# A fused spectral-mixing and GeGLU kernel: loads of x shared between two issuing engines, new instruction orders, and a separate key for the last half tile

## The chip, the cores and the metric

The kernel runs on one core of a Trainium2 chip. The metric is the time of one execution on the device, in microseconds (us). Three runs of the kernel before took 491.49, 491.52 and 491.66 us (median 491.52). A profile of one execution gives the start and length of the instructions on each engine: TensorE (PE, with its weight loads as PEld), VectorE (DVE), ScalarE (ACT), GpSimd (POOL) and SyncE (SP, which here only starts transfers).

## What is computed

```python
h  = x + irfft2(rfft2(layernorm(x)) * (w_r + 1j * w_i))        # over tokens and channels
h2 = h + (gelu(layernorm(h) @ w_gate) * (layernorm(h) @ w_up)) @ w_down
```

x has 2048 tokens of 576 channels in bf16; w_gate and w_up are 576 x 4608, w_down is 4608 x 576. The layer norms have no weights. The Fourier transforms are done as matrix products with cos/sin tables that are constants of the program.

## The kernel before

The 2048 tokens lie in 16 tiles of 128 rows (c = 0 to 15; token 16p + c is row p of tile c). The work goes through these stages, and TensorE goes from one to the next.

**Stage A** (tokens to frequencies, first factor). Tile by tile, x is loaded (`x_load`), its mean and variance are taken, and the transform's table is multiplied by 1/std, so that the matmuls need no normalized x. The tiles are handled in six groups, `GROUPS` (line 23): tiles 0-1, 2-3, 4-6, 7-9, 10-12, 13-15. For a group the chain is:

- statistics of each tile: on DVE two half-tile `bn_stats` (tokens `B` and `b` in the order list, line 480) and then `bn_aggr` (`v`, line 489); for tiles 3, 4 and 13 on ACT instead, a sum (`S`, line 472) and a sum of squares (`Q`, line 476), with the mean squared by a small instruction `m` (line 483) on POOL or DVE;
- the square root on ACT (`q`, line 496) and the reciprocal on DVE (`c`, line 501);
- the scaled table ATS = ATB * 1/std (`x`, line 506 on POOL or 511 on DVE);
- a negated copy of the upper half of x (`n`, line 553) and a copy of its middle (`t`, line 558), both on POOL;
- the matmuls (`M`, line 537; 9 for each tile) and their evictions from PSUM to U (`E`, and `F` for the second half of a split one, line 548).

The order of all these instructions is written by hand in one list, `SEQ1` (line 24). Each token emits its instructions on one engine (the ending A, D or P names ACT, DVE or POOL), and each engine runs its own in the order in which they stand in the list and waits in place for what an instruction needs. `k` tokens are idle matmuls on zeros.

**The loads** come ahead of it, in the order of `LORD` (line 25): `x0-2` loads tiles 0 and 1 of x, `a0-4` tiles 0 to 3 of the table ATB. All are issued by SP. A trailing `@` would have ACT issue one (line 434); no entry has it. After them SP issues FT and BT, the spectral weights WS (22 transfers), VT and the tables of later stages, and then feed-forward weights. ACT's first instruction is a small square root (line 431, key `("SA0", 0)`), for which it loads its table.

**Stages D, B, T, Z, V, R** (the channel transform, the spectral product and the way back) go over 16 groups of frequencies in the order `SEQF` (line 28): D and B are matmuls with an eviction on ACT, `w` and T and Z the products on DVE, V and R matmuls with evictions on ACT and DVE. **Stages I and N** bring six token tiles back and add them to x; squares, reciprocals, the normalized HN (`n`, `e`), the transposes by PE (`A` evicted by ACT, `D` by DVE, `z` by both) and the first pieces of the gate and up products (`g`, `h`) are ordered by `SEQ` (line 31). `I` has its eviction on ACT, and `J` is an `I` with its eviction on DVE; `S` is the square on DVE and `s` the same on ACT.

**The feed-forward** goes over four blocks of 512 tokens: `gu_part` (line 877, gate and up) and then `down` (line 978) for the block's four tiles. `down` does a tile in two pieces of columns, 0-288 and 288-576, for the last tile 0-448 and 448-576. Each piece is 36 matmuls, one addition on DVE into OS (line 981) and one store by SP (line 983). OS has two buffers, used in turn.

Dependencies are found by keys: an instruction names the keys that it reads and writes, and `emit` (line 226) makes a wait for each earlier instruction on another engine, or on its own (except PE), that it has to follow. An instruction with two waits has one of them as a separate instruction in its queue (line 288). In the last tile the first addition writes the keys `("OS", 1, 0)` and `("OS", 1, 1)`, since 448 columns reach over the usual border of 288; the second writes `("OS", 1, 1)`.

Of the kernel before, what the change touches and what calls it, by code (L numbers as in the profile page):

```python
# [9 lines left out]
S, D, K2 = 2048, 576, 289  # L10
# [5 lines left out]
NT = 16  # L16
# [296 lines left out]
def _build(nc, A_x, A_w_r, A_w_i, B_w_gate, B_w_up, B_w_down, out):  # L313
    P = Prog(nc)
    T = build_tables()
    dram = {n: nc.inline_tensor(_np_bf16(T[n]), name="c_" + n.lower()) for n in T}
    PE, DVE, ACT, SP, POOL = "pe", "dve", "act", "sp", "pool"
# [4 lines left out]
    XO = sb.alloc("XO", [128, NT, D], BF16)  # L322
# [645 lines left out]
    def down(tb, p):  # L968
        c = 4 * tb + p

        cut = 448 if c == NT - 1 else 288
        for h, (d0, d1) in enumerate(((0, cut), (cut, D))):
            b = 2 * (tb > 0 and p % 2 == 0) + h
            for k, f in enumerate([*range(36)] if tb == 0 else [*range(9, 36), *range(9)]):
                if tb == 0:
                    for fn in DEF.get(72 * p + 36 * h + k, ()):
                        fn()
                P.op(PE, lambda t, b=b, d0=d0, d1=d1, f=f, p=p: t.matmul(bank(b, 0, 128, 0, d1 - d0), AT[:, f, 128 * p:128 * p + 128],  # L978
                                                                        WD[:, f, d0:d1], start=(f == 9 * (tb > 0)), stop=(f == (8 if tb else 35))),
                     r=[("AT", f), ("WD", f // 4)], w=[("PS", b)])  # L980
            P.op(DVE, lambda v, b=b, d0=d0, d1=d1, p=p, c=c: v.tensor_tensor(OS[:, p % 2, d0:d1], bank(b, 0, 128, 0, d1 - d0), XO[:, c, d0:d1], op=ALU.add),  # L981
                 r=[("PS", b), ("X", c)], w=[("OS", p % 2, k) for k in (range(2) if d1 == cut and cut > 288 else (h,))])
            P.dma(SP, ov[:, c, d0:d1], OS[:, p % 2, d0:d1], f"so{p % 2}{h}", r=[("OS", p % 2, h)], w=[("OUT", p % 2, h)])
# [65 lines left out]
```

## Time and profile before

| what | value |
|---|---|
| median of three runs | 491.52 us |
| the profiled execution | 491.4 us, its span in the profile 489.6 us |
| PE busy | 482.3 us (99% of the span) |
| ACT, DVE, POOL busy | 151.4, 192.8, 32.9 us |
| granted TensorE clock | 1.00 throughout |
| stage A's last run of matmuls | 15.00 to 19.84 us |
| D, B, V, R matmuls | 19.84 to about 48 us |
| I, N and the transposes | 48.04 to 58.95 us |
| feed-forward | 58.95 to 486.64 us |
| end of the last addition | 487.38 us |

Landing of the first loads, each from its issue and the time from issue to landing that the transfer view gives:

| load | issued | lands after | landed |
|---|---|---|---|
| x0-2 (288 KB) | 0.73 | 2.9 | 3.63 |
| x2-4 (288 KB) | 1.18 | 3.2 | 4.38 |
| a0-4 (128 KB) | 1.64 | 3.0 | 4.6 |
| x4-8 (576 KB) | 2.11 | 5.4 | 7.52 |
| a4-8 (128 KB) | 2.58 | 6.0 | 8.6 |
| x8-12 (576 KB) | 3.06 | 7.1 | 10.2 |
| x12-16 (576 KB) | about 3.5 | 8.1 | 11.6 |
| a8-16 (256 KB) | 4.01 | 8.3 | 12.3 |
| FT (432 KB) | 4.70 | 9.2 | 13.9 |

Times in the profile are counted from the start of the span. In a row of the timeline the first number is the start, the second the length; the bracket at the end tells how long the engine was idle before it and what ended that. The chain of waits follows the work that ended last back to its start.

### The profile page before, as it was taken

What the parts mean: (1) busy time and instruction counts of PE and PEld (TensorE: products, weight loads), DVE (VectorE), ACT (ScalarE), POOL (GpSimd) and SP (SyncE); (2) the same over time, 40 slices, a digit from 0 to 9 for tenths busy, and PEclk for the clock granted to TensorE, in tenths of its full rate; (3) what the DMA queues carried; (4) which work ended last, traced back from release to release, by engine and by line L of the source; (5) the groups of instructions that cost most, each with busy time, mean ns of one, the idle gap of its engine ahead of it and who ended that gap; (6) DMA issues with size and microseconds to landing.
All of it is one profiled execution on the core that took longest, in us unless ns stands there. A gap on an engine that the chain in (4) does not pass through costs nothing.

```text
span 489.6 us, 9943 instructions
## 1 busy us (share of the span) xinstructions
PE 482.3 (99%) x4376; PEld 286.2 (58%) x4376; DVE 192.8 (39%) x392; ACT 151.4 (31%) x297; POOL 32.9 (7%) x67
## 2 busy tenths in 40 slices
PE   7999999999999999999999999999999999999997
PEld 3887754444688744444577644444677444444774
DVE  6799733433576534433311144333211233333101
ACT  6999742332322223233200022332100123223000
POOL 6411431000000020000000000000000000000000
PEclk9999999999999999999999999999999999999999
DMA  8991999000001071100000001000000000000000
GB/s 289 224 328 20 365 362 345 19 15 2 1 19 40 14 233 26 23 2 1 2 18 19 13 20 23 15 1 0 7 19 19 7 1 0 1 2 1 13 19 19
DMA packets 25148, 31.20 MB, mean 64 GB/s; under 512 B 11440, under 2 KB 17840, under 8 KB 25104
## 3 DMA queue, kind: packets, MB, share of 16 engines
q1 hardware_dynamic: 22208, 18.62, 13.4%
q0 software_dynamic: 2896, 11.95, 7.0%
q8 instruction: 34, 0.56, 0.5%
q14 instruction: 10, 0.08, 0.1%
HBM read 26.22 MB, written 2.36 MB: 58 GB/s over the span
## 4 chain that ended last, share of the span: by engine, by line
PE 96%; DVE 1%; DMA 1%; ACT 0%; SPq 0%; issue 0%; POOL 0%; DVEq 0%
PE PS L877 57%; PE PS L978 29%; PE PS L611 2%; PE PS L621 2%; PE PS L651 1%; DMA XO<-in_A_x_dram 1%; PE PS L895 1%; PE PS L537 1%; PE PS L736 1%; DVE ST L480 1%; PE PS L779 1%; PE PS L913 1%; PE PS L841 0%; SPq L223 0%; PE PS L663 0%
## 5 line engine op out<-in xcount | busy, mean ns | idle before, releaser
L877 PE MATMUL PS<-HT,WG 64*128 64x512 bf16 (+1 forms) x2160 | 228.7, 371 | 0.0
L877 PEld LDWEIGHTS PS<-HT,WG 64*128 64x128 bf16 x2160 | 104.7, 94 | 122.2 <-issue 0.7
L886 DVE TENSOR_TENSOR AT<-GL,PS 128x512 bf16<-128x512 bf16 (+1 forms) x147 | 99.4, 677 | 177.9 <-ACT GL L885 177.9
L885 ACT ACTIVATE GL<-PS 128x512 bf16<-128x512 f32 (+1 forms) x147 | 86.5, 589 | 262.6 <-PE PS L877 251.3
L978 PE MATMUL PS<-WD,AT 128*128 128x288 bf16 (+2 forms) x1152 | 144.9, 286 | 0.0
L978 PEld LDWEIGHTS PS<-WD,AT 128*128 128x128 bf16 x1152 | 110.7, 98 | 30.6 <-ACT GL L885 1.3
L877 PE MATMUL PS<-HT,WGX 64*128 64x512 bf16 x486 | 53.4, 376 | 0.0
L981 DVE TENSOR_TENSOR OS<-PS,XO 128x288 bf16<-128x288 f32 (+2 forms) x32 | 14.6, 457 | 94.8 <-PE PS L978 94.7
L877 PEld LDWEIGHTS PS<-HT,WGX 64*128 64x128 bf16 x486 | 23.7, 94 | 28.8
L611 PE MATMUL PS<-FT,U 128*128 128x288 bf16 x96 | 13.9, 286 | 0.0
L630 DVE TENSOR_TENSOR TP<-YS,WS 128x1152 bf16<-128x1152 bf16 (+2 forms) x17 | 12.0, 718 | 2.8 <-ACT YS L603 2.6
L900 ACT ACTIVATE EB<-PS 128x288 f32<-128x288 f32 x10 | 4.1, 411 | 27.7 <-PE PS L895 27.7
L480 DVE BATCH_NORM_STATS2 ST<-XO 128x6 f32<-128x288 bf16 x26 | 10.0, 440 | 3.6 <-DMA XO<-in_A_x_dram 3.6
L918 DVE TENSOR_TENSOR XO<-PS,XO 128x576 bf16<-128x576 f32 x10 | 7.6, 756 | 8.0 <-PE PS L913 8.0
L537 PE MATMUL PS<-ATS,XO 128*128 128x128 bf16 x96 | 8.5, 219 | 2.3 <-POOL ATS L506 2.3
L611 PEld LDWEIGHTS PS<-FT,U 128*128 128x128 bf16 x96 | 9.3, 98 | 2.4
L603 ACT ACTIVATE CUS<-PS 128x576 bf16<-128x576 f32 x16 | 10.5, 654 | 0.5
L603 ACT ACTIVATE YS<-PS 128x576 bf16<-128x576 f32 x16 | 10.4, 654 | 0.1
L621 PE MATMUL PS<-CUS,BT 128*128 128x288 bf16 x64 | 10.3, 286 | 0.0
L548 ACT ACTIVATE U<-PS 128x384 bf16<-128x384 f32 (+2 forms) x29 | 9.5, 429 | 0.2
L906 DVE TENSOR_TENSOR QB<-PS,EB 128x288 f32<-128x288 f32 x20 | 8.2, 452 | 3.3 <-ACT EB L900 3.3
L823 DVE TENSOR_SCALAR HN<-XO,NM,RS 128x576 bf16<-128x576 bf16 (+1 forms) x28 | 9.2, 369 | 0.1
(79 smaller groups left out, 208.0 us busy)
## 6 DMA issues: line engine op xcount, KB each, us to landing
WD<-in_B_w_down_dram POOLq DMA_DIRECT2D x9, 576.0 KB, 12.2
WG<-in_B_w_up_dram SPq DMA_DIRECT2D x4, 1152.0 KB, 8.0
WG<-in_B_w_gate_dram POOLq DMA_DIRECT2D x4, 1152.0 KB, 10.3
out_dram<-OS SPq DMA_DIRECT2D x30, 72.0 KB, 1.6
XO<-in_A_x_dram SPq DMA_DIRECT2D x3, 576.0 KB, 7.1
WGX<-in_B_w_up_dram SPq DMA_DIRECT2D x1, 1152.0 KB, 6.0
WGX<-in_B_w_gate_dram POOLq DMA_DIRECT2D x1, 1152.0 KB, 9.5
HT<-HN SPq DMA_TRANSPOSE x60, 2.4
```

Source lines behind the costliest of these rows:

```text
L480: P.op(DVE, lambda v: v.bn_stats(ST1[:, c, h, :], XO[:, c, 288 * h:288 * h + 288]), r=[("X", c)], w=[("ST1", c, h)])
L537: P.op(PE, lambda t, b=b, lhs=lhs, s=s, e=e, o=o, c=c: t.matmul(bank(b, 0, 128, o, o + 128), lhs, ATS[:, c, :], start=s, stop=e), r=[("X", ...
L548: fn = (lambda v: v.tensor_copy(dst, src)) if eng == DVE else (lambda a: a.activation(dst, src, ACTF.Copy))
L603: fn = (lambda v: v.tensor_copy(dst, src)) if eng == DVE else (lambda a: a.activation(dst, src, ACTF.Copy))
L611: P.op(PE, lambda t, b=b, m=m, us=us, o=o: t.matmul(bank(b, 0, 128, 0, 2 * HK), U[:, us, i, :, :], FT[:, 3 * o + (2 if us == 4 else us // ...
L621: P.op(PE, lambda t, b=b, tb=tb, m=m, s3=s3, sp_=sp_: t.matmul(bank(b, 0, 128, 0, KW), BT[:, sp_, tb, :], CUS[:, s3, m, :], start=(m == 0) ...
L630: P.op(DVE, lambda v: v.tensor_tensor(TP[:, tl, :, :, q0:q1], y4, w4, op=ALU.mult), r=[("Y", sl), ("Wn", i)] + (wkeys[0] if 1 <= g < 9 els ...
L877: op = P.op(PE, lambda t, h0=h0, kt=kt, wt=wt, b=b, s=(not second and j == 0), e=(second and j == n - 1): t.matmul(bank(b, 0, 128, c0, c1) ...
L885: P.op(ACT, lambda a: a.activation(GL[:, s2, c0:c1], bank(b0, 0, 128, c0, c1), ACTF.Gelu_apprx_tanh), r=[("PS", b0)], w=[("GL", s2)])
L886: P.op(DVE, lambda v: v.tensor_tensor(AT[:, f, c0:c1], GL[:, s2, c0:c1], bank(b0 + 1, 0, 128, c0, c1), op=ALU.mult), r=[("GL", s2), ("PS", ...
L978: P.op(PE, lambda t, b=b, d0=d0, d1=d1, f=f, p=p: t.matmul(bank(b, 0, 128, 0, d1 - d0), AT[:, f, 128 * p:128 * p + 128], WD[:, f, d0:d1], ...
L981: P.op(DVE, lambda v, b=b, d0=d0, d1=d1, p=p, c=c: v.tensor_tensor(OS[:, p % 2, d0:d1], bank(b, 0, 128, 0, d1 - d0), XO[:, c, d0:d1], op=A ...
```

## The change

The loads are in a new order, and three of the eight (x4-8, a4-8, x12-16) are issued by ACT. Such a load now reads the key `("SA0", 0)`, so ACT issues it after its first square root. A mark `!` is understood as well and isn't used. `SEQ1`, `SEQF` and `SEQ` are new orders of nearly the same tokens. In `SEQ1` the small instruction of tile 3 goes from POOL to DVE (`m3P` to `m3D`), `t2` comes ahead of `x0P`, and evictions are dealt out anew between ACT and DVE. In `SEQ` `I3` becomes `J3`, `S1` becomes `s1`, and the four transposes `z0 D1 D2 z3` become `D0 A1 D2 A3`. In `down` the last tile's second piece has a key of its own, `("OS", 1, 2)`.

```diff
--- before.py
+++ after.py
@@ -21,14 +21,14 @@
 NPRE = 6
 PARTS = ((0, 256), (256, 512))
 GROUPS = ((0, 2), (2, 4), (4, 7), (7, 10), (10, 13), (13, 16))
-SEQ1 = """t1 n0 b0 k104 S3 m3P k14 n1 B1 b1 b2 t0 B0 v0 q0 c0 x0P t2 Q3 B2 v1 q1 c1 S4 B5 M0 b5 b6 Q4 x1P E0A E1A M1 B6 m4P v2 b7 q2 E2A E8A B7 E6A E5A c2 n2 n3 E3A E9A B8 E7A E4A b8 B9 b11 k202 b9 v3 x2P b10 M2 Q13 q3 S13 B10 t3 E13A c3 b12 n4 E10A B11 B12 v4 E11A q4 B15 c4 E14A b14 x3P M3 E15A B14 E12A m13P E17A b15 E18A v5 E16D q5 c5 x4P x5D t4 E19A n5 t5 M4 E22D E20A E23A F23D E24D E21A M5 E25A E26A F25A E28A F22D E27D E29A F24D F26D F28D F27A F29A""".split()
-LORD = "x0-2 x2-4 a0-4 x4-8 a4-8 x8-12 x12-16 a8-16".split()
+SEQ1 = """k14 B1 b0 S3 n0 B0 t0 b1 v0 k104 b2 B2 n1 t1 t2 q0 c0 x0P Q3 n2 M0 m3D b6 b5 Q4 S4 b7 E0A E1A m4P B5 v1 q1 B6 B8 E3A v2 B9 c1 q2 b8 S13 n3 b11 E2A x1P M1 B7 c2 Q13 E4A E5A b9 v3 B11 B10 m13P q3 c3 b12 x2P b10 E7A E8A E6A E9A k202 M2 E10A E11A B12 v4 b14 n4 x3P t3 q4 c4 x4P B15 E12A E13A t4 B14 M3 b15 v5 E15A E14A E16A q5 n5 E18A M4 E17D c5 x5D E20A E19A E24A E23D E21D F23A F24A t5 E22A M5 E27A E25D E26D F25D E28A E29A F29D F27A F26A F22A F28D""".split()
+LORD = "x0-2 a0-4 x2-4 x8-12 a8-16 x4-8@ a4-8@ x12-16@".split()
 SPLIT = tuple(int(w[1:-1]) for w in SEQ1 if w[0] == "F")
 ACT_TILES = tuple(int(w[1:]) for w in SEQ1 if w[0] == "Q")
-SEQF = """D0 w0 D2 D1 B0 D3 B1 w1 D4 T0 Z0 T1 B2 T2 B3 D6 D5 Z2 B4 D7 Z1 T3 Z3 B5 V0 T4 B6 w2 Z4 D8 T5 R0 V1 D9 T6 B7 D10 Z6 B8 V2 T7 B9 Z5 T8 V3 B10 D11 w3 Z7 T10 V6 V5 Z10 T9 D12 R1 B11 D13 V4 Z8 B12 Z9 T11 D14 T12 Z11 B13 V7 Z12 B14 D15 T13 T14 V8 V9 Z13 Z14 B15 R2 T15a T15b V10 V13 V14 Z15a V11 V12 Z15b R3 V15 R4""".split()
+SEQF = """w1 D1 D0 D2 B1 B0 D3 w0 D4 T0 B2 Z0 T1 D5 T2 Z2 B3 D6 T3 Z3 B5 Z1 w2 B4 T4 D7 V0 Z4 B6 D8 V1 T5 B7 T6 B8 Z6 V3 V2 D9 T7 Z7 Z5 R0 D10 T8 w3 B9 D12 R1 D11 T9 B10 T10 V4 B11 D13 Z9 Z8 B12 V6 D14 T11 T12 B13 Z11 V5 Z10 V7 B14 Z12 D15 T13 T14 V8 Z13 V9 Z14 B15 R2 V10 T15a T15b Z15a V13 V11 Z15b V12 V14 R3 V15 R4""".split()
 VENG = [('act',), ('act',), ('act',), ('act',), ('act',), ('act',), ('act',), ('act',), ('act',), ('act',), ('act',), ('act',), ('act',), ('act',), ('act',), ('act', 'act')]
 DENG, BENG = ['act', 'act', 'act', 'act', 'act', 'act', 'act', 'act', 'act', 'act', 'act', 'act', 'act', 'act', 'act', 'act'], ['act', 'act', 'act', 'act', 'act', 'act', 'act', 'act', 'act', 'act', 'act', 'act', 'act', 'act', 'act', 'act']
-SEQ = """I0 I1 N0 I2 s0 N1 I3 S1 q0 N2 I4 c0 e0 s2 q1 n0 n1 N3 I5 c1 z0 n2 s3 e1 D1 N4 N5 e2 q2 c2 n3 e3 D2 g10 g00 h10 z3 h00 g20 g01 h20 h01 g21 g11 h21 h11""".split()
+SEQ = """I0 I1 N0 I2 N1 J3 s0 s1 q0 N2 c0 e0 n1 I4 n0 s2 q1 N3 I5 D0 c1 n2 e1 A1 N4 e2 N5 s3 q2 c2 n3 D2 g00 g10 e3 h00 A3 g20 h10 g11 h20 h11 g01 g21 h01 h21""".split()
 QR0 = ((0, 2), (2, 3), (3, 4))
 QR = QR0 + ((4, NPRE), (NPRE, 8), (8, 16))
 DSTEP, DLAG, ALAG = 288 // (16 - NPRE), 24, 26
@@ -422,16 +422,16 @@
     ov = out[0].rearrange("(p c) d -> p c d", c=NT)
     tabs = dram["ATAB"].rearrange("p (c k) -> p c k", c=NT)
 
-    def x_load(i, c0, c1, eng):
-        P.dma(eng, XO[:, c0:c1, 0:D], xv[:, c0:c1, :], f"ld{i}", w=[("X", c) for c in range(c0, c1)])
-
-    def atb_load(i, c0, c1, eng):
-        P.dma(eng, ATB[:, c0:c1, :], tabs[:, c0:c1, :], f"ld{i}", w=[("ATB", c) for c in range(c0, c1)])
+    def x_load(i, c0, c1, eng, r):
+        P.dma(eng, XO[:, c0:c1, 0:D], xv[:, c0:c1, :], f"ld{i}", r=r, w=[("X", c) for c in range(c0, c1)])
+
+    def atb_load(i, c0, c1, eng, r):
+        P.dma(eng, ATB[:, c0:c1, :], tabs[:, c0:c1, :], f"ld{i}", r=r, w=[("ATB", c) for c in range(c0, c1)])
 
     P.op(ACT, lambda a: a.activation(SA[:, 0, 0:1], EPT[:, 0:1], ACTF.Sqrt), r=["EPT"], w=[("SA0", 0)])
     for i, w in enumerate(LORD):
-        c0, c1 = (int(v) for v in w[1:].rstrip("@").split("-"))
-        (x_load if w[0] == "x" else atb_load)(i, c0, c1, ACT if w[-1] == "@" else SP)
+        c0, c1 = (int(v) for v in w[1:].rstrip("@!").split("-"))
+        (x_load if w[0] == "x" else atb_load)(i, c0, c1, ACT if w[-1] in "@!" else SP, {"@": [("SA0", 0)], "!": [("X", 0)]}.get(w[-1], []))
     P.dma(SP, FT[:, :, :].rearrange("p a b -> p (a b)"), dram["FTAB"][:, :], "ft", w=["FT"])
     P.dma(SP, BT[:, :, :, :].rearrange("p a b c -> p (a b c)"), dram["BTAB"][:, :], "bt", w=["BT"])
 
@@ -979,8 +979,8 @@
                                                                         WD[:, f, d0:d1], start=(f == 9 * (tb > 0)), stop=(f == (8 if tb else 35))),
                      r=[("AT", f), ("WD", f // 4)], w=[("PS", b)])
             P.op(DVE, lambda v, b=b, d0=d0, d1=d1, p=p, c=c: v.tensor_tensor(OS[:, p % 2, d0:d1], bank(b, 0, 128, 0, d1 - d0), XO[:, c, d0:d1], op=ALU.add),
-                 r=[("PS", b), ("X", c)], w=[("OS", p % 2, k) for k in (range(2) if d1 == cut and cut > 288 else (h,))])
-            P.dma(SP, ov[:, c, d0:d1], OS[:, p % 2, d0:d1], f"so{p % 2}{h}", r=[("OS", p % 2, h)], w=[("OUT", p % 2, h)])
+                 r=[("PS", b), ("X", c)], w=[("OS", p % 2, k) for k in ((0, 1), (2,))[h]] if c == NT - 1 else [("OS", p % 2, h)])
+            P.dma(SP, ov[:, c, d0:d1], OS[:, p % 2, d0:d1], f"so{p % 2}{h}", r=[("OS", p % 2, 2 * h if c == NT - 1 else h)], w=[("OUT", p % 2, h)])
 
 
     P.alias(fdead, fnew)
```

## The prediction

> **What bounds the kernel now.** I read the chain of waits first. It is PE nearly throughout, so only what lies ahead of PE's unbroken run, or behind its last matmul, can change the time:
>
> ```profile
> 2.11 5.41 DMA XO<-in_A_x_dram
> ...
> 14.12 0.84 POOL ATS L506
> 14.95 0.05 issue
> 15.00 4.84 PE PS L537 x81
> 19.84 2.21 PE PS L611 x18
> ...
> 486.64 0.03 issue
> 486.67 0.02 DVEq L288
> 486.69 0.40 issue
> 487.09 0.29 DVE OS L981
> ```
>
> From 15.00 PE runs without a gap to about 46.5, loses about half a microsecond there, and from 58.95 is busy to 486.64. The release of that run is the scaled table of group 3 (`x3P`), ready at 14.95. So the question of stage A is when `x3P` ends. In the chain a DVE instruction stands ahead of it, but POOL's own timeline shows that POOL itself was full (start, length, what):
>
> ```profile
> 7.98 0.27 POOL L558 TENSOR_SCALAR XN<-XO 128x96 bf16<-128x96 bf16 x1 [0.16 <-POOL ATS L506]
> 8.40 0.61 POOL L506 TENSOR_TENSOR ATS<-ATB,RS 128x256 bf16<-128x256 bf16 x1
> 9.19 0.26 POOL L483 TENSOR_SCALAR TM<-SA 128x1 f32<-128x1 f32 x1 [0.18 <-POOL ATS L506]
> 9.54 0.91 POOL L553 TENSOR_SCALAR XN<-XO 128x864 bf16<-128x864 bf16 x1
> 10.60 0.91 POOL L553 TENSOR_SCALAR XN<-XO 128x864 bf16<-128x864 bf16 x1 [0.15 <-POOL XN L553]
> 11.69 0.83 POOL L506 TENSOR_TENSOR ATS<-ATB,RS 128x384 bf16<-128x384 bf16 x1 [0.17 <-POOL XN L553]
> 12.60 0.27 POOL L558 TENSOR_SCALAR XN<-XO 128x96 bf16<-128x96 bf16 x1
> 13.03 0.91 POOL L553 TENSOR_SCALAR XN<-XO 128x864 bf16<-128x864 bf16 x1 [0.15 <-POOL XN L558]
> 14.12 0.83 POOL L506 TENSOR_TENSOR ATS<-ATB,RS 128x384 bf16<-128x384 bf16 x1 [0.17 <-DVE ST L480]
> ```
>
> The steps from start to start are the costs: `t` of three tiles 0.42, `x` of two 0.79, `m` 0.35, `n` of three 1.06 to 1.09, `x` of three 0.91 with the step and 0.83 alone. Then the windows of half a microsecond (last two columns DMA share and GB/s) for the loads:
>
> ```profile
> 3.50:4.00 0.50, 0.50 (x3) 0.15 (x2) 0.37 (x1) 0.00 (x0) 0.00 (x0) 1.00 0.99 370
> 4.00:4.50 0.50, 0.50 (x3) 0.22 (x2) 0.50 (x3) 0.12 (x1) 0.06 (x1) 1.00 1.36 217
> 4.50:5.00 0.50, 0.50 (x3) 0.22 (x2) 0.50 (x2) 0.50 (x2) 0.34 (x2) 1.00 0.44 138
> 5.00:5.50 0.50, 0.50 (x3) 0.15 (x2) 0.50 (x2) 0.15 (x2) 0.50 (x1) 1.00 0.85 313
> ```
>
> The transfers run at about 395 GB/s from 2.5 on, but between about 4.25 and 5.0, just ahead of x4-8, they nearly stop.
>
> **The change: loads.** Call L the landing of x4-8 and T that of x12-16 (7.52 and 11.6 before). SP issues five loads instead of eight. ACT is free from 2.22 (its square root ends) until x2-4 lands at 4.4, and three issues at 0.43 each (the length of SP's) end at about 3.6, so they cost ACT nothing. If x2-4 were there at once, they would cost 1.3. x4-8 is issued at about 2.3 instead of 2.11, x8-12 at 2.11 instead of 3.06, x12-16 at 3.2 instead of 3.5; x2-4 comes one place later, lands about 0.3 later and isn't waited for by then. FT and all behind it go out some 1.5 earlier; FT had landed at 13.9 and is used at 19.84, DT landed at 27 and is used at 48, so nothing is gained there.
>
> L is not in the trace. From below: the first three loads (0.72 MB) have moved by 4.25, x4-8 (0.59 MB) at 395 GB/s takes 1.5 more, and x0-2 and x2-4 landed 0.5 behind their last bytes: 6.2. From above: x4-8 and x8-12 go in equal turns and end together, where x8-12 landed before (10.2), less a4-8's 0.35: 9.8. I take 6.9: x0-2, first in an idle queue, reached full rate 1.8 after its issue, so x4-8 on ACT's queue would at 4.1, right for the gap; 0.30 MB pass alone until 5.0, the remaining 0.29 MB at half rate take 1.45, and 0.5 until landing. T from below: all 2.62 MB of x and table from 2.5 at 395 GB/s, plus 0.5, is 9.7; from above the 11.6 of before. Less 0.3 for the earlier issue and 0.55 for the 0.215 MB that the gap lost, it is 10.75; x12-16 has fewer pieces ahead in its queue, and I take 10.5.
>
> **The order of stage A.** On POOL `t2`, which needs x4-8, now stands ahead of `x0P`; behind it come `n2 m4P n3 x1P m13P x2P n4 x3P`. What waits behind `t2` on POOL is thus the scaling of every group. From L: 0.42 + 0.79 + 1.06 + 0.35 + 1.09 + 0.79 + 0.35 + 0.91 + 1.09 + 0.83 = 7.68. With L = 6.9, `x3P` ends at 14.58. A second wait is new: `m13P` now stands ahead of `x2P` and needs ACT's sum of tile 13, 0.82 plus about 0.1 from T; the rest from `m13P` on is 3.18, so `x3P` can't end ahead of T + 4.1 = 14.6. On ACT that sum `S13` stands ahead of `q3`; behind it come three evictions (0.29 each, 8 in 2.28 in ACT's timeline), `Q13` (0.85), `q3` (0.3) and DVE's `c3` (0.1): `x3P` could start at T + 0.85 + 0.87 + 0.85 + 0.4 + 0.05, and end 0.83 later, T + 3.85, within the former. DVE: it starts at 3.63, and up to `x5D` (ended 18.32) sat idle for 0.36, 0.36, 0.23 and 0.41. The new order fills these, adds `m3D` (0.15) and waits from 6.4 to L: 3.63 + 13.33 + 0.15 + 0.5 = 17.6, so it isn't last unless L is over 7.6. So `x3P` ends at 14.6 instead of 14.95, and the 81 matmuls, 4.84, follow as before: **-0.35**.
>
> **Orders of the other stages.** PE does the same matmuls. In D to V it was gapless up to 46.5, and ACT is busy 4.8 to 5.0 of each 5 us there, with the same evictions. What could be gained is the half microsecond near 47; what could be lost is, by the nearest row, one eviction late (0.65). In I and N the eviction of `J3` (0.65) goes to DVE and the square `s1` to ACT; each engine gives about what it takes, and PE's idle there adds up to some 0.3. I take 0, with -0.4 and +0.6 as ends.
>
> **The last half tile.** The second addition had to wait for PE and, by its key, for the first addition, on its own engine and long done. The chain shows PE's wait released at 486.67 and the addition 0.40 after it. An ordinary half, with a wait for PE and one for an old store, has nothing of it; its wait event and its addition stand at the same time:
>
> ```profile
> L288 DVEq EVENT_SEMAPHORE  x1: 21/21/21, 477.9 to 477.9; - x1
> ...
> 477.92 0.46 DVE L981 TENSOR_TENSOR OS<-PS,XO 128x288 bf16<-128x288 f32 x1 [3.95 <-PE PS L978]
> ```
>
> With the new key only PE's wait is left. Bounds: 0 if the 0.40 has another cause, -0.42 at most. I take the row of the ordinary half: **-0.4**. The store and its landing follow unchanged.
>
> **Sum:** -0.35 + 0 - 0.4 = -0.75. The profiled execution took 491.4 (span 489.6), giving 490.65; the median of the runs is 0.12 above it, so **490.8**.
>
> **Rivals.**
> - *All lands early.* L 6.2 and T 9.8: `x3P` ends at 13.9, -1.05, with -0.4: **490.1**. For it: the gap is there to be filled, and POOL, ACT and DVE would be free for x4-8 at 6.15 to 6.7 in the new order. Against it: x8-12 moves at the same time.
> - *The queues share.* x4-8, at the head of POOL's order, gets only every other turn beside x8-12, and the gap is not filled, as WGX shows: alone, issued at 171.33, it too got to full rate only 2.4 later. L is 9.4, `x3P` ends at 17.1, +2.15 - 0.4: **493.3**, slower than before. It decides against the change from L = 7.7 on, and by over 0.2% from L = 8.7. Against it: x0-2 was at full rate 1.8 after issue.
> - *x12-16 is late.* T stays at 11.6, because FT now moves beside it: `x3P` ends at 15.7, +0.75 - 0.4: **491.9**.
> - *The 0.40 at the end stays*, since it isn't the own wait: **491.2**.
>
> The Trainium skill (DMA: Bandwidth & Descriptors, Issuing engines are not separate DMA queues) says that transfers from all engines run on the same 16 DMA engines, and several issuers save only the issue time; the same page (Queues, rings and completion order) lets each DMA engine take turns between queues. By that rule the second rival is right and the change is slower. That the DMA share is 1.0 from 5.0 on agrees with it; no run here shows two such queues at once.
>
> **Chances.** Forecast (490.3 to 491.3) 0.36, all early 0.32, queues share 0.11, x12-16 late 0.12, the 0.40 stays 0.09. 0.2% is 0.98 us, about what a measurement of this kernel can tell from no change. Faster by more: all of the early case and 0.10 of the forecast, 0.42. Slower by more: most of the sharing case, 0.09. Within: 0.49. The range goes from 489.8 (early, with 0.3 from the orders) to 492.2 (x12-16 late, with 0.3 lost in the orders) and leaves out the sharing case's bulk.
>
> **What would show it.** L between 6.5 and 7.3 and `t2` on POOL at L; `x3P` ending near 14.6 and 81 gapless matmuls behind it; no DVEq wait at the end and the last addition within 0.05 of PE's end; the span from the first D matmul to 58.95 still 39.1. POOL waiting for x4-8 past 7.7, or ACT's `S13` past 11, would make the prediction wrong.

## The result and the profile after

| kernel | median of runs, us | lowest to highest | against before |
|---|---|---|---|
| before | 491.52 | 491.49 to 491.72 | |
| after | 495.70 | 494.71 to 496.49 | 1.0084 [1.0073, 1.0095] |

The change makes the kernel 4.2 us slower, where 0.7 faster was forecast. The profiled execution took 496.49 (span 494.5), 5.09 above that of before. It is the longest of the five runs after, and the spread between runs is itself new: 1.8 us, against 0.2 before.

The chain of waits of the kernel after, the long pieces (start, length, what):

```profile
2.26 8.43 DMA XO<-in_A_x_dram
...
15.14 2.10 PE PS L537 x18
17.24 0.85 PE PS L522 x2
18.09 7.17 PE PS L537 x108
25.27 2.21 PE PS L611 x18
...
456.77 35.40 PE PS L978 x288
```

and the end of the same chain:

```profile
492.17 0.02 issue
492.20 0.29 DVE OS L981
```

Three sums give the loss up to the last addition. Stage A ends (first `L611`) at 25.27 instead of 19.84: **+5.43**. From there to the feed-forward it takes 39.21 (to 64.48) instead of 39.11: **+0.10**. The last addition comes 0.03 after PE instead of 0.45: **-0.42**. Together 5.11. Behind the last addition the span ends 1.97 later instead of 2.23, as the last store lands sooner, and 2.03 instead of 1.79 of the execution's time lie outside the span; these two nearly cancel, which leaves the 5.09. So all of the loss is in stage A, and the head of the chain names it: the load of x4-8 takes 8.43 and lands at 10.69 instead of 7.52.

POOL's timeline of the kernel after, where the scaled tables are made (start, length, what; in brackets the idle time before and what ended it):

```profile
7.17 0.67 POOL L553 TENSOR_SCALAR XN<-XO 128x576 bf16<-128x576 bf16 x1 [2.21 <-DMA XO<-in_A_x_dram]
...
10.76 0.27 POOL L558 TENSOR_SCALAR XN<-XO 128x96 bf16<-128x96 bf16 x1 [2.59 <-DMA XO<-in_A_x_dram]
...
16.31 0.26 POOL L483 TENSOR_SCALAR TM<-SA 128x1 f32<-128x1 f32 x1 [1.22 <-ACT JNK L472]
...
18.74 0.83 POOL L506 TENSOR_TENSOR ATS<-ATB,RS 128x384 bf16<-128x384 bf16 x1 [0.17 <-POOL XN L553]
```

Three waits that were not there before: for x2-4 (`n1`, until 7.17), for x4-8 (`t2`, until 10.76) and for ACT's sum of tile 13 (`m13P`, 1.22), which is x12-16 landing at 15.4. `x3P` ends at 19.57 instead of 14.95.

What the waits do to PE is seen in its timeline and in the windows of 2 us (busy time of PE, PEld, DVE, ACT, POOL, each with its count, then the granted clock, DMA share and GB/s):

```profile
11.88 0.29 PE L537 MATMUL PS<-ATS,XO 128*128 128x128 bf16 x1 [3.78 <-POOL ATS L506]
```

```profile
8.00:10.00 2.00, 0.10 (x1) 0.00 (x0) 0.28 (x2) 0.74 (x3) 0.17 (x1) 1.00 1.02 368
10.00:12.00 2.00, 0.12 (x2) 0.13 (x3) 1.29 (x4) 1.29 (x4) 0.98 (x3) 0.53 1.01 403
12.00:14.00 2.00, 1.98 (x18) 1.71 (x16) 2.00 (x11) 1.51 (x7) 1.67 (x3) 0.50 1.12 282
14.00:16.00 2.00, 0.86 (x9) 0.86 (x10) 2.00 (x10) 0.73 (x2) 0.94 (x2) 0.50 1.08 203
16.00:18.00 2.00, 2.00 (x16) 1.40 (x15) 0.47 (x4) 2.00 (x9) 1.43 (x3) 0.50 1.11 202
18.00:20.00 2.00, 2.00 (x21) 2.00 (x20) 1.72 (x8) 1.93 (x8) 1.67 (x3) 0.50 1.11 221
20.00:22.00 2.00, 2.00 (x36) 2.00 (x34) 1.88 (x8) 1.75 (x6) 1.45 (x3) 0.91 1.12 209
```

PE stood idle for 3.78 us; about 2 us into that the granted clock fell from 1.00 to 0.50 and stayed there until about 20.4. The matmuls of that time step at 0.11 us (18 in 1.98) instead of 0.06 (108 in 6.03 at full clock, below). Before, PE's longest idle stretch in stage A was 1.53 and the clock stayed at 1.00.

So there are two candidates behind the late load, the new order of the list and the second queue, and a second effect, the clock. The experiments take these apart.

### The profile page after: what moved, and what is told of

Read it like the earlier page. It is cut to its first block, busy times and chain, and to the rows that moved or that the text cites. A ratio compares the mean times of both kernels' runs of the same rounds, so it can differ in the third digit from the quotient of the medians.

```text
span 494.5 us, 9933 instructions
## 1 busy us (share of the span) xinstructions
PE 485.5 (98%) x4376; PEld 288.8 (58%) x4376; DVE 192.7 (39%) x389; ACT 151.9 (31%) x299; POOL 32.8 (7%) x66
## 3 DMA queue, kind: packets, MB, share of 16 engines
q1 hardware_dynamic: 21776, 17.31, 12.8%
## 4 chain that ended last, share of the span: by engine, by line
PE 94%; ACT 2%; DMA 2%; POOL 1%; issue 0%; DVE 0%; POOLq 0%
PE PS L877 57%; PE PS L978 29%; PE PS L611 2%; PE PS L537 2%; DMA XO<-in_A_x_dram 2%; PE PS L895 1%; PE PS L621 1%; ACT V L603 1%; PE PS L736 1%; ACT YS L603 1%; PE PS L779 1%; PE PS L913 0%; ACT CUS L603 0%; PE PS L651 0%; POOL XN L553 0%
## 5 line engine op out<-in xcount | busy, mean ns | idle before, releaser
L981 DVE TENSOR_TENSOR OS<-PS,XO 128x288 bf16<-128x288 f32 (+2 forms) x32 | 14.6, 457 | 94.4 <-PE PS L978 94.3
L537 PE MATMUL PS<-ATS,XO 128*128 128x128 bf16 x96 | 11.0, 256 | 4.9 <-POOL ATS L506 4.9
L611 PE MATMUL PS<-FT,U 128*128 128x288 bf16 x96 | 13.9, 286 | 0.0
L480 DVE BATCH_NORM_STATS2 ST<-XO 128x6 f32<-128x288 bf16 x26 | 10.2, 442 | 7.7 <-DMA XO<-in_A_x_dram 7.7
L537 PEld LDWEIGHTS PS<-ATS,XO 128*128 128x128 bf16 x96 | 8.7, 118 | 6.1 <-POOL ATS L506 6.1
L603 ACT ACTIVATE CUS<-PS 128x576 bf16<-128x576 f32 x16 | 10.5, 660 | 0.8 <-PE PS L611 0.5
L611 PEld LDWEIGHTS PS<-FT,U 128*128 128x128 bf16 x96 | 9.3, 98 | 2.3
L548 ACT ACTIVATE U<-PS 128x256 bf16<-128x256 f32 (+2 forms) x30 | 10.1, 409 | 0.9 <-PE PS L537 0.6
L603 ACT ACTIVATE YS<-PS 128x576 bf16<-128x576 f32 x16 | 10.2, 660 | 0.2 <-DVE TP L630 0.2
## 6 DMA issues: line engine op xcount, KB each, us to landing
XO<-in_A_x_dram ACTq DMA_DIRECT2D x2, 576.0 KB, 10.3
```

The costliest lines, as they stand in the source:

```text
L480: P.op(DVE, lambda v: v.bn_stats(ST1[:, c, h, :], XO[:, c, 288 * h:288 * h + 288]), r=[("X", c)], w=[("ST1", c, h)])
L537: P.op(PE, lambda t, b=b, lhs=lhs, s=s, e=e, o=o, c=c: t.matmul(bank(b, 0, 128, o, o + 128), lhs, ATS[:, c, :], start=s, stop=e), r=[("X", ...
L548: fn = (lambda v: v.tensor_copy(dst, src)) if eng == DVE else (lambda a: a.activation(dst, src, ACTF.Copy))
L603: fn = (lambda v: v.tensor_copy(dst, src)) if eng == DVE else (lambda a: a.activation(dst, src, ACTF.Copy))
L611: P.op(PE, lambda t, b=b, m=m, us=us, o=o: t.matmul(bank(b, 0, 128, 0, 2 * HK), U[:, us, i, :, :], FT[:, 3 * o + (2 if us == 4 else us // ...
```

## The experiments

Landings first, since most runs are read by them (issue plus time to landing in the transfer view; where it is fuller, from the waits of those that need the load):

| kernel | x2-4 | x4-8 | x8-12 | x12-16 |
|---|---|---|---|---|
| before | 4.4 | 7.5 | 10.2 | 11.6 |
| after | 7.1 | 10.7 | 10.5 | 15.4 |
| after_warm | 6.6 | 9.7 | 9.5 | 13.5 |
| loads_only | 6.7 | 9.05 | 8.6 | 12.8 |
| one_queue | 6.2 | 10.5 | 8.1 | 12.4 |
| late_on_act | 4.3 | 8.8 | 11.0 | 14.2 |

The landings of one list differ between executions: the kernel after, `after_warm` (the same with more idle matmuls, see below) and `loads_only` have the same loads, and x4-8 landed at 10.7, 9.7 and 9.05. The trace records 16 landings for each load, one for each part of it, and a wait for the load ends with the last of them. In the profiled execution of the kernel after, one part was about 1 us behind the others: 15 parts of x4-8 had landed by 9.69 and the last at 10.69, of x8-12 by 9.50 and at 10.52, of x12-16 by 14.07 and at 15.40. In `after_warm` the last two parts of x4-8 landed at 9.63 and 9.67. So about 1 us of the latest landings is one slow part of that execution, and the rest is common to all three.

**1. The four parts alone.** `loads_only` is the kernel before with the new `LORD` and the ACT issues. `orders_only` is the kernel after with the old loads. `key_only` is the kernel before with the new key of the last half tile. `one_queue` is the kernel after with the new order of the list, all of it issued by SP:

```diff
 loads_only:  before, and
-LORD = "x0-2 x2-4 a0-4 x4-8 a4-8 x8-12 x12-16 a8-16".split()
+LORD = "x0-2 a0-4 x2-4 x8-12 a8-16 x4-8@ a4-8@ x12-16@".split()
 orders_only: after, and
-LORD = "x0-2 a0-4 x2-4 x8-12 a8-16 x4-8@ a4-8@ x12-16@".split()
+LORD = "x0-2 x2-4 a0-4 x4-8 a4-8 x8-12 x12-16 a8-16".split()
 key_only:    before, and the new lines of down
-w=[("OS", p % 2, k) for k in (range(2) if d1 == cut and cut > 288 else (h,))]
+w=[("OS", p % 2, k) for k in ((0, 1), (2,))[h]] if c == NT - 1 else [("OS", p % 2, h)]
 one_queue:   after, and
-LORD = "x0-2 a0-4 x2-4 x8-12 a8-16 x4-8@ a4-8@ x12-16@".split()
+LORD = "x0-2 a0-4 x2-4 x8-12 a8-16 x4-8 a4-8 x12-16".split()
```

Expected of `loads_only`:

> The kernel before with only the loads changed (new order of loads, three of them issued by ACT); orders and key as before. Theory S (two queues share): the loads alone bring the whole loss. x2-4 lands near 7.1 and x4-8 near 10.7 as in the changed kernel; in the old order POOL has t2, x1P, m4P, n2, n3, x2P, t3, n4, x3P behind x4-8, 6.96 us, so x3P ends near 17.7 instead of 14.95, and with half a microsecond or more for a lowered PE clock the run is 3 to 4.5 slower: 494.5 to 496. Rival O (the new orders lose): within 0.5 of the kernel before, 491 to 492.

Expected of `orders_only`:

> The changed kernel with the old loads, all issued by SP in the old order; the three new orders and the new key stay. Theory S: x4-8 lands near 7.5 and x12-16 near 11.6 again, x3P ends between 15.2 and 15.7, PE's clock stays at full speed, 0.4 is won at the end: 491.1 to 491.9. Rival O: t2 ahead of x0P and the squares of tile 4 ahead of q1 lose by themselves: 494 or more.

Expected of `key_only`:

> The kernel before with only the key of the last half tile. All theories: the last addition starts within 0.05 of the end of PE's last matmul instead of 0.45 after it, and the time is 0.4 lower: 491.1. If the 0.40 had another cause it is 491.5.

Expected of `one_queue`:

> The changed kernel with its eight loads in the same order of the list, but all issued by SP. Theory S: without a second queue x2-4 lands by 4.8 and not at 7.1, x4-8 (behind 1.57 MB) near 10.4, x12-16 near 12.3 and not at 15.4, so x3P ends near 18.1 instead of 19.6 and the time is 493.5 to 494.5. Rival P (only the place in the list counts): x2-4 and x4-8 land as in the changed kernel and the time is the same, 495.7.

| kernel | median, us | against before |
|---|---|---|
| loads_only | 494.50 | 1.0062 [1.0047, 1.0077] |
| orders_only | 493.31 | 1.0034 [1.0021, 1.0047] |
| key_only | 490.78 | 0.9987 [0.9977, 0.9996] |
| one_queue | 495.75 | 1.0087 [1.0072, 1.0102] |

*The loads alone* cost 3.0 us. *The orders alone* (with the key's gain inside) cost 1.8. *The key alone* gains 0.74 and is the only part that gains; the end of its chain shows how:

```profile
486.72 0.02 issue
486.75 0.29 DVE OS L981
```

The wait event of DVE's queue is gone, and the last addition starts 0.03 after PE's end instead of 0.45. Its last store then landed in 1.5 us, where that of before took 1.7; that is the rest of its span's 0.6. The key goes with it: the last store takes 1.4 or 1.5 in each kernel with the new key whose end was read, and 1.7 in `loads_only` and `table_first`, which have the old one. Why that is so stays open.

*One queue* is as slow as two (495.75 and 495.70). The profiled executions lie 1.36 apart, but that of `one_queue` was the fastest of its four and that of the kernel after the slowest of its five. x4-8 and x12-16 landed as theory S of its expectation had them, and the time is that of rival P. So issuing from ACT isn't the cause by itself: with the list in its new order on SP alone, x4-8 stands behind x8-12 and a8-16 (0.85 MB) and lands at 10.5 all the same. POOL's timeline of `one_queue`:

```profile
10.60 0.27 POOL L558 TENSOR_SCALAR XN<-XO 128x96 bf16<-128x96 bf16 x1 [3.30 <-DMA XO<-in_A_x_dram]
```

`orders_only` fits neither of its expectations: it lost 1.8, and its clock fell. The clock falls in three of these runs. In `loads_only` PE's idle stretch of 3.33 has it at 0.50 from 11.0 to 14.4, and in `one_queue` one of 3.25 from 10.9 to 17.7. In `orders_only` no idle stretch is over 2.23, but two follow each other with 1.2 us of matmuls between (PE's timeline, then windows of that kernel):

```profile
9.08 0.23 PE L537 MATMUL PS<-ATS,XO 128*128 128x128 bf16 x1 [2.23 <-POOL ATS L506]
...
12.34 0.29 PE L537 MATMUL PS<-ATS,XO 128*128 128x128 bf16 x1 [2.08 <-POOL ATS L506]
```

```profile
9.00:11.00 2.00, 1.18 (x18) 1.01 (x18) 1.63 (x9) 1.47 (x6) 1.58 (x4) 1.00 1.02 410
11.00:13.00 2.00, 0.66 (x7) 0.66 (x8) 2.00 (x10) 1.45 (x5) 1.40 (x3) 0.50 1.04 393
13.00:15.00 2.00, 2.00 (x16) 1.54 (x14) 1.65 (x9) 2.00 (x9) 1.74 (x2) 0.50 1.11 233
```

**2. The clock held, and the parts of the orders.** `after_warm` and `orders_warm` are the kernel after and `orders_only` with more idle matmuls (`k` tokens; the last two digits are their number), placed in the stretches where PE waits, so that it isn't idle. `late_orders` is the kernel before with the new key, `SEQF` and `SEQ`, but the old `SEQ1` and loads. `table_first` is the kernel before with only the first table piece ahead of x2-4:

```diff
 after_warm:  in SEQ1 of after
-k104 ... M0 ... k202
+k122 ... M0 k110 ... k206
 orders_warm: in SEQ1 of orders_only
-k104 ... M0 ... k202
+k114 ... M0 k110 ... k203
 late_orders: after, with SEQ1 and LORD of before
 table_first: before, and
-LORD = "x0-2 x2-4 a0-4 x4-8 a4-8 x8-12 x12-16 a8-16".split()
+LORD = "x0-2 a0-4 x2-4 x4-8 a4-8 x8-12 x12-16 a8-16".split()
```

Expected of `after_warm`:

> The changed kernel with more idle matmuls on zeros where PE stood idle in stage A (18 more ahead of M0, 10 between M0 and M1, 4 more ahead of M2), so that PE's clock is not lowered; nothing else is changed. Theory S with a clock part: the clock stays at 1.00, the two half-speed groups shrink, evictions and so q4, q5 come earlier, and 0.4 to 1.0 of the 4.2 comes back: 494.7 to 495.3. If the lowered clock were most of the loss: under 493.5. If it cost nothing: 495.7.

Expected of `orders_warm`:

> The changed kernel with the old loads (as in the run with the orders alone), with idle matmuls added in the same places (10 ahead of M0, 10 between M0 and M1, 1 ahead of M2). Theory C (with the old loads the new orders lose through PE's lowered clock): the clock stays at 1.00, 1.0 to 1.8 of the loss of 1.8 comes back: 491.5 to 492.3. Rival O (the order of stage A itself is slow): 493.0 to 493.5, with a clock of 1.00.

Expected of `late_orders`:

> The kernel before with the new key and the two later orders (SEQF and SEQ); loads and SEQ1 as before. All theories but one: within 0.3 of the run with the key alone, 490.6 to 491.1. If the later orders carry part of the loss: above 491.2.

Expected of `table_first`:

> The kernel before with one pair of loads swapped: the table a0-4 ahead of x2-4, all issued by SP. Theory G (what is moving when the transfers slow down near 4.2 pays for it, in whichever queue): x2-4 lands near 6.3 instead of 4.4, POOL's first instruction t1 waits for it and the chain behind it is up to 1.9 late: 492 to 493.5. Rival (x2-4 was late because of x8-12 and the second queue): x2-4 lands by 4.9 and the time is 491.4 to 491.9.

| kernel | median, us | against before |
|---|---|---|
| after_warm | 494.86 | 1.0069 [1.0052, 1.0085] |
| orders_warm | 492.19 | 1.0016 [1.0006, 1.0025] |
| late_orders | 491.19 | 0.9996 [0.9987, 1.0005] |
| table_first | 493.09 | 1.0033 [1.0022, 1.0043] |

In both warm kernels the clock stays at 1.00 throughout. By the medians *the clock is worth 0.8 us in the kernel after* (495.70 to 494.86) and 1.1 in `orders_only` (493.31 to 492.19). The two profiled executions can't confirm the 0.8, since x4-8 landed 1.0 earlier in `after_warm` and `x3P` ended at 17.95 instead of 19.57, which is all of the 1.57 between them. The trace of the kernel after gives the price in another way: `x3P` ended at 19.57, and 0.05 + 4.84 later, as before, stage A would have ended at 24.46; it ended at 25.27, 0.81 later, because the matmuls of group 2 ran at half speed until 20.4. That is little for the 10 and 7 us at half speed: up to the end of `x3P` PE mostly waits for POOL, and time is lost only by the matmuls that run late for it.

POOL's timeline of `orders_warm` shows the new order of stage A with the old loads:

```profile
7.54 0.27 POOL L558 TENSOR_SCALAR XN<-XO 128x96 bf16<-128x96 bf16 x1 [1.75 <-DMA XO<-in_A_x_dram]
...
12.04 0.26 POOL L483 TENSOR_SCALAR TM<-SA 128x1 f32<-128x1 f32 x1 [0.18 <-ACT U L548]
...
14.47 0.83 POOL L506 TENSOR_TENSOR ATS<-ATB,RS 128x384 bf16<-128x384 bf16 x1 [0.17 <-DVE ST L480]
```

`t2` starts when x4-8 has landed (7.5), and `x3P` ends at 15.30: 7.8 later, against the 7.68 of the prediction's sum. So that sum holds, and so does its consequence: with L = 7.5 the new order ends 0.35 later than the old one. In the profiled execution of `orders_warm` stage A's matmuls end at 20.29, 0.45 later than before (chain, next lines):

```profile
14.26 6.03 PE PS L537 x108
20.29 2.20 PE PS L611 x18
```

Against `late_orders` it is 0.54 there, and 1.0 by the medians: the ten runs of `orders_warm` spread from 491.6 to 493.2, those of `late_orders` from 491.1 to 491.5, and the profiled one was among the fastest. The likely reason is that the new `SEQ1` turns variations of the landings into time, which the old one, with POOL's list full of work that needs only earlier pieces, does not; the runs that were not profiled can't show it.

`late_orders` against `key_only` gives +0.4 by the medians for the later orders, a little over what was expected. The stages that were reordered hold hardly any of it: the stretch between stage A and the feed-forward takes 39.21 against 39.12, and the spans of the ten runs of each kernel have the same median, 489.0. The 0.4 lies outside the profile's span, which is 2.1 to 2.2 shorter than the execution in every run of `late_orders` and 1.75 to 1.8 in every run of `key_only`; in the other kernels with the new later orders it is 1.8 to 2.1. What takes that time is open. Inside the span the new order is seen in the chain of `late_orders`, in which ACT now takes turns with PE:

```profile
35.83 0.75 PE PS L611 x6
36.58 0.02 issue
36.60 0.51 ACT CUS L603
37.11 0.04 issue
37.15 0.65 ACT YS L603
```

`table_first` shows that one change of place suffices: a0-4 ahead of x2-4 costs 1.6 us, with one queue and everything else as before. x2-4 lands at 5.85 instead of 4.38. In DVE's timeline of `table_first`, the fourth half-tile statistic (`b2`, of tile 2) waits for it, where before DVE did five in a row from 3.63 on:

```profile
3.63 1.18 DVE L480 BATCH_NORM_STATS2 ST<-XO 128x6 f32<-128x288 bf16 x3 [3.63 <-DMA XO<-in_A_x_dram]
5.88 0.82 DVE L480 BATCH_NORM_STATS2 ST<-XO 128x6 f32<-128x288 bf16 x2 [1.07 <-DMA XO<-in_A_x_dram]
```

From 5.88 everything on DVE is 1.2 to 1.5 later than before, and `x3P` ends at 16.44 instead of 14.95.

**3. Other ways to share the loads, and the place of `t2`.** `late_on_act` and `tables_on_act` have the old orders and the new key; the first puts only late pieces on ACT, the second only the tables. `t2_behind` is `orders_warm` with `t2` back behind `x0P`. In a last run, `x_first`, again with the old orders and the new key, SP alone issues all, with x4-8 ahead of the first table:

```diff
 late_on_act:   old orders, new key, and
+LORD = "x0-2 x2-4 a0-4 x4-8 a8-16 a4-8@ x8-12@ x12-16@".split()
 tables_on_act: old orders, new key, and
+LORD = "x0-2 x2-4 x4-8 x8-12 x12-16 a0-4@ a4-8@ a8-16@".split()
 t2_behind:     in SEQ1 of orders_warm
-t2 q0 c0 x0P
+q0 c0 x0P t2
 x_first:       old orders, new key, and
+LORD = "x0-2 x2-4 x4-8 a0-4 a4-8 x8-12 x12-16 a8-16".split()
```

Expected of `late_on_act`:

> Old orders and the new key; SP issues x0-2, x2-4, a0-4, x4-8, a8-16 and ACT issues a4-8, x8-12, x12-16, so that x4-8 keeps its old place and only what is needed later goes to ACT's queue. To be set beside the run with the key alone, 490.8. Theory S (two queues take turns): x8-12 moves beside x4-8, which lands at 8.5 to 9 instead of 7.5, ACT's square and DVE's statistics of tiles 4 to 6 wait for it, 491.8 to 492.8. Rival G (only the place in the order counts, not the queue): x4-8 lands by 7.8 and the time is 490.6 to 491.1.

Expected of `tables_on_act`:

> Old orders and the new key; SP issues the five pieces of x in order and ACT the three tables a0-4, a4-8, a8-16. Theory S: a0-4 takes turns with x4-8, lands by 6.5, ahead of its use at 7.2, and x4-8 lands between 7.2 and 8: 490.5 to 491.3. If a second queue as such costs something: above 491.5. If it brings something: below 490.4.

Expected of `t2_behind`:

> The changed kernel with the old loads and the added idle matmuls (492.2), and with t2 behind x0P on POOL as in the kernel before. Theory (POOL's chain from the landing of x4-8 is what the new stage A costs with the old loads): x0P starts near 6.5 instead of 8.0, x3P ends 0.6 to 0.8 earlier, 491.4 to 491.7. Rival (the landing of x12-16, or ACT's order with q3 and q4 behind S13 and Q13, holds it): 492.0 to 492.4.

Expected of `x_first`:

> Old orders and the new key, all loads issued by SP, with x4-8 directly behind x2-4 and the table a0-4 behind it. Theory G2 (the slow stretch of the transfers comes with the table's rows of 1 KB, not at a fixed time): x4-8 is moved at full rate and lands by 6.6 instead of 7.5, and the slow stretch comes behind it; a0-4 lands between 6.8 and 8 and is used at 7.2: 490.5 to 491.5 beside 490.8 with the key alone. Rival (the transfers are slow from 4.2 to 5.0 whatever is moved): x4-8 lands at 7.2 or later.

| kernel | median, us | against before |
|---|---|---|
| late_on_act | 492.41 | 1.0018 [1.0009, 1.0028] |
| tables_on_act | 494.88 | 1.0060 [1.0043, 1.0076] |
| t2_behind | 492.17 | 1.0011 [1.0002, 1.0021] |
| x_first | 491.32 | 0.9998 [0.9989, 1.0008] |

The base of three of these is `key_only`, 490.78. *Neither way of sharing gained*: late pieces on ACT cost 1.6 against it, tables on ACT 4.1, far above what was expected of it. The chain of `late_on_act` begins with x12-16, third in ACT's queue:

```profile
3.14 11.06 DMA XO<-in_A_x_dram
...
14.22 0.78 ACT JNK L476 x2
```

It lands at 14.2, 2.6 later than before, and x4-8, in SP's queue, at 8.8, as the pieces on ACT's take turns from it. In `tables_on_act` the x pieces land as early as before or earlier (x4-8 7.5, x8-12 9.5, x12-16 11.3), but the first table, 128 KB, takes 8.16 and lands at 10.41. POOL's first scaling in `tables_on_act` waits for it:

```profile
10.49 0.61 POOL L506 TENSOR_TENSOR ATS<-ATB,RS 128x256 bf16<-128x256 bf16 x1 [3.48 <-DMA ATB<-c_atab]
```

PE stood idle for 4.20 there, and its clock was at 0.50 from 11.2 to 14.6.

The transfer view shows how the queues share (q1 is SP's, q10 is ACT's; packets, MB, share of 16 engines). First `tables_on_act` from 6 to 7 us and from 9 to 10, then the kernel after from 7 to 8:

```profile
q1 hardware_dynamic: 46, 0.19, 68.3%
q10 hardware_dynamic: 24, 0.02, 13.0%
```

```profile
q1 hardware_dynamic: 80, 0.30, 74.2%
q10 hardware_dynamic: 82, 0.08, 23.1%
```

```profile
q1 hardware_dynamic: 62, 0.20, 52.2%
q10 hardware_dynamic: 62, 0.15, 45.1%
```

Once both are at work, the two queues move about the same number of packets, not of bytes. ACT's queue is slow to come to that: in `tables_on_act` it moved 4 packets from 5 to 6, 24 from 6 to 7 and 43 from 7 to 8, against 70, 46 and 62 of SP's. So much of the first table's 8.16 is this slow start. A packet here is about one row of a load: 0.08 MB / 82 is 1 KB (a row of a table piece), 0.30 MB / 80 is 3.7 KB. So a load of short rows beside one of long rows gets a quarter of the bytes, and a load of equally long rows half. The total doesn't rise: 373 GB/s in that window of `tables_on_act`, against 370 to 421 in the better half-microseconds before.

*What the queues share* was the second rival. The Trainium skill (DMA: Bandwidth & Descriptors, Queues, rings and completion order) has each DMA engine take turns between its queues, a packet at a time. The 62 and 62 packets agree with it. By that page a packet is some 9 to 17 descriptors. The profile's packets are of 1 KB and 3.7 KB on average, about a row each; its counts can't tell how many of them pass at a turn, only that the two queues get equally many.

*The place of `t2`* costs nothing: 492.17 against 492.19. POOL's timeline of `t2_behind` shows what is there instead:

```profile
10.33 0.91 POOL L553 TENSOR_SCALAR XN<-XO 128x864 bf16<-128x864 bf16 x1 [0.86 <-DMA XO<-in_A_x_dram]
11.52 0.61 POOL L506 TENSOR_TENSOR ATS<-ATB,RS 128x256 bf16<-128x256 bf16 x1 [0.27 <-DVE RS L501]
```

`n3` needs x8-12 (10.2) and stands ahead of `x1P`, and `x1P` needs DVE's `c1`, behind `B8`, which needs x8-12 too. The new `SEQ1` asks for x8-12 in two places ahead of group 1's table. So its cost with the old loads isn't in one token.

*`x_first`* doesn't beat `key_only` (491.32 against 490.78): x4-8 landed at 7.35, only 0.3 earlier than in `key_only` (7.64) and where the rival had it, and the first table at 7.7. But the slow stretch of the loads, which the prediction read at 4.25 to 5.0, did not stay at that time. Windows of `x_first`:

```profile
4.50:5.00 0.50, 0.50 (x3) 0.23 (x2) 0.50 (x3) 0.50 (x1) 0.30 (x2) 1.00 0.91 369
5.00:5.50 0.50, 0.50 (x3) 0.15 (x2) 0.50 (x2) 0.26 (x2) 0.50 (x1) 1.00 0.92 222
5.50:6.00 0.50, 0.50 (x2) 0.15 (x1) 0.45 (x3) 0.00 (x0) 0.32 (x2) 1.00 1.04 170
6.00:6.50 0.50, 0.50 (x2) 0.15 (x1) 0.15 (x2) 0.48 (x2) 0.42 (x2) 1.00 0.83 198
6.50:7.00 0.50, 0.50 (x3) 0.25 (x2) 0.47 (x3) 0.48 (x2) 0.42 (x2) 1.00 0.81 277
```

370 GB/s (last column) until 5.0, then 170 to 280 for 2 us. In `table_first`, with the table one place earlier, it is 249 to 290 from 3.0 to 4.5; in `tables_on_act` 201 to 298 from 5.5 to 7.5, with work waiting in both queues. So the gap is not a time in which one queue is empty and that another could fill.

The table's 1 KB rows are not slow by themselves. Before, the slowest window (4.5 to 5.0, 138 GB/s) moved 15 rows of 4.6 KB and none of the table; a row of the table took 0.046 us from 3.5 to 4.5, and one of x2-4, of 2.3 KB, 0.093. What took long were the first rows of x4-8: the 10 that started from 4.0 to 4.5 took 0.80 us each on average, where a row of that length otherwise takes 0.18. And `loads_only`, with the very loads of the kernel after, moved 318 to 415 GB/s from 4.0 to 7.0, where that moved 249 to 336. What can be seen is that a few of a load's 16 parts fall behind: of x4-8 in `x_first` 13 had landed by 5.87 and the others at 6.64, 6.93 and 7.33; in `tables_on_act` 13 by 5.72, the others from 6.56 to 7.58; of x2-4 in the kernel after 13 by 5.22, the others from 6.54 to 7.09. Why they do is open.

`key_only` is the fastest of all kernels that ran, by 0.13% against before, with an interval that leaves out 1 just so.

## Why the prediction was wrong

**The sum of the loss.** By the medians: the key -0.75, the later orders +0.4 (`late_orders` less `key_only`), the new `SEQ1` with the old loads +2.1 (`orders_only` less `late_orders`; 1.1 of it the clock), the new loads on top +2.4 (after less `orders_only`). Together 4.2, the measured difference. Each term is the step from one kernel to the next, so the total is no test, and the split hangs on the order of the steps: put on the kernel before, the loads cost 3.0.

**The step that failed: L and T.** The prediction took x4-8 at 6.9, with bounds 6.2 to 9.8, and x12-16 at 10.5, with bounds 9.7 to 11.6. They landed at 10.7 and 15.4 in the profiled execution, both beyond the upper bound; the same loads in `after_warm` and `loads_only` put them at 9.7 and 9.05, and at 13.5 and 12.8. So x4-8 is 2.2 to 3.8 later than the value taken in all three, and T is over its bound in all three. What is behind L and T held: from L, 10.69 + 7.68 = 18.4; from T, 15.4 + 4.1 = 19.5; `x3P` ended at 19.57. By the prediction's own arithmetic, with the measured landings, the profiled execution would have been 491.4 + 4.55 - 0.4 = 495.6. It was 496.49, and the 0.81 by which half speed held up group 2's matmuls is most of the rest.

*Why 6.9 was wrong.* It let 0.30 MB of x4-8 pass alone until 5.0 and the rest at half of 395 GB/s. Neither came. ACT's queue moved its first packets only in the microsecond from 4 to 5 (17 of them, 0.08 MB, against 75 of SP's), 2 us after its issue. From 5 on it had about half of the packets, and both queues together moved only 279 to 352 GB/s until 9, when x4-8's rows were nearly through. 15 of its parts had landed by 9.69, the last at 10.69.

*Why the upper bounds were wrong.* That for L, 9.8, let x4-8 and x8-12 end together, and they did: all but one part of each had landed by 9.50 and 9.69. What the bound had no room for is the one slow part, 1.0 later; in the two other kernels with these loads L lay within it. That for T was the old landing; but behind x8-12 SP's queue goes on with a8-16, FT and the spectral weights, and x12-16, last of ACT's 1.3 MB, shared the engines with them: from 9 to 12 SP's queue moved 85, 67 and 111 packets in a microsecond and ACT's 83, 69 and 41. From 13 to 15 ACT's had 2 in each against 189 and 206, the last rows of x12-16; its slow part landed 1.3 behind the other 15. FT landed at 15.1, x12-16 at 15.4. The lower bound of T was too low as well: its 2.62 MB leave out a8-16, 0.26 MB, which the new list puts ahead of x12-16, and with it the same sum gives 10.3. "FT and all behind it go out some 1.5 earlier" stood in the prediction as a gain of nothing; it was the price. The third rival had the reason ("because FT now moves beside it") and then left T at 11.6.

**"x2-4 lands about 0.3 later and isn't waited for by then."** It landed 2.7 later, at 7.1, and POOL waited 2.21 and DVE 1.44 for it. Here x4-8 came later still and hid that; with one queue, `table_first` shows that such a swap alone costs 1.6.

**The rival at 0.11.** "The queues share" was the right mechanism, priced at 493.3 for L = 9.4. The rows spoke for it more than the chance said: the DMA share was 1.0 from 5.0 on, and WGX, the only load alone in a queue in the middle of the kernel, got to full rate 2.4 after issue. The one row against it, x0-2 at full rate 1.8 after issue, was the first load, with nothing in flight. And `one_queue` shows that the rival was only half of it: the new order of the list does the same without any sharing.

**What was not thought of: the clock.** The prediction counted matmuls at the step of the trace before, 81 in 4.84, in which PE never idled for over 1.53. A late load makes PE idle, and the idle time is paid a second time in half speed: 0.8 us here, 1.1 in `orders_only`. The Trainium skill (TensorE: Matmul & The Clock Gate, Why this matters for your kernels) warns of idle stretches over some 3 us between matmuls. The kernel after, `loads_only` and `one_queue` agree, with 3.78, 3.33 and 3.25. `orders_only` lost the clock with none over 2.23, so there the measurement is stricter than the rule; what the traces show to count is the idle time in each stretch of 3.41 us of a fixed grid (last section).

**What was right.** The last half tile, -0.42 in the chain against -0.4; but "the store and its landing follow unchanged" was not so, the store landed 0.2 to 0.3 sooner as well. The chain on POOL (7.68; 7.8 measured with L = 7.5) and the bound from T. The orders of the other stages, 0 with +0.6 as the end: 0.1 in the chain. The 0.4 by the medians lies outside the span, for which the prediction had no term; that the end of +0.6 covers it is luck. The warning signs were the right ones, "POOL waiting for x4-8 past 7.7, or ACT's `S13` past 11": both came, at 10.76 and 15.42.

## What to carry to other kernels

Loads that are limited by the DMA engines, as these are, gained nothing from a second issuing queue: it takes turns from the first by packets, so what was last in the one long list now also delays what was first; order the list by first need, and count what follows in the *other* queue as traffic beside the load. A landing under a new order is a size to bound from the far side with everything that is in flight, by packets and not by bytes, and with room for a part that falls behind. And when a wait ahead of TensorE grows, price its clock too: look at the granted clock of the windows, and keep PE busy with idle matmuls where it must wait.

## What the runs showed of the hardware that was not expected

- Two queues that are both at work share by nearly equal counts of packets: 62 and 62 in the kernel after, 80 and 82 with 0.30 and 0.08 MB in `tables_on_act`. ACT's queue moved its first packet 1.5 to 3.2 us after its first issue at about 2.26 (at 3.74 in `after_warm`, 4.27 in the kernel after, 5.41 in `tables_on_act`).
- A load is as late as the last of its 16 parts, of which a few can fall behind. One part was 1.0 to 1.3 behind the other 15 in x4-8, x8-12 and x12-16 of the kernel after; three of 16 were 0.8 to 1.9 behind in x4-8 of `x_first` and `tables_on_act` and in x2-4 of the kernel after. The rate of the loads falls to 140 to 290 GB/s for 1 to 2 us early in the kernel (before, `x_first`, `table_first`, `tables_on_act`), not always at the same time nor always with table rows in motion. The cause is open.
- In the eleven traces that have a record of TensorE's granted clock, it changed only on a grid of 3.41 us: its stretches at 0.50 in stage A lasted 3.41 (`loads_only`, `tables_on_act`), 6.83 (`one_queue`, `orders_only`) and 10.24 (the kernel after). It fell behind grid stretches in which PE was idle (neither a matmul nor a weight load running) for 2.03 us (the kernel after), 2.23 (`orders_only`), 2.40 (`one_queue`), 2.56 (`loads_only`) and 3.34 (`tables_on_act`), and not behind one of 1.83 (`x_first`) or less. It came back behind stretches with up to 0.69 of idle time (`one_queue`) and not behind 1.16 (the kernel after). So in `orders_only` two idle stretches counted together, 1.48 and 0.75 of them lying between 7.60 and 11.01, while `table_first`, whose stretch of 2.23 the grid divides into 1.05 and 1.18, kept the clock.
- A DVE addition with a wait for its own long-finished predecessor beside PE's started 0.45 after PE's end, without it 0.03 after, in each of the kernels with the new key whose end was read (after, `key_only`, `late_orders`).
